# A second MoE layer's first tile: its tokens gathered from three of four batches, and the first half of its first product placed among the routing

## The chip, the cores and the metric

The kernel runs on one core of a Trainium2 chip. The metric is device time in microseconds (us), the median of several executions. The core has five instruction queues that matter here: PE (TensorE, matmuls and transposes), ACT (ScalarE), DVE (VectorE), POOL (GpSimd, which also issues the indirect gathers and scatters) and SP (SyncE, which issues all other transfers).

## The reference

Attention over four batches of 448 tokens (12 heads of 64, queries and keys normalised), then a dense two-layer MLP, called the first MoE here, then a routed MoE with eight experts:

```python
def _moe_ref(x, w_in, w_out):
    h = x @ w_in
    g = np.maximum(0.01 * h, h)
    return g @ w_out

def _moe2_ref(x, w_gate, w_output_gate, w1, w2):
    logits = x @ w_gate
    e_idx = np.argmax(logits, axis=1)
    probs = softmax(logits)
    gate_w = probs[np.arange(N), e_idx]
    eom = sigmoid(x @ w_output_gate)
    for e in range(E):
        mask = e_idx == e
        h = np.maximum(x[mask] @ w1[e], 0.0)
        out[mask] = gate_w[mask, None] * eom[mask, e, None] * (h @ w2[e])
    return out
```

There are 1792 tokens of width 768, and w1 and w2 are 768 x 1024 and 1024 x 768 for each expert.

## The kernel before, in words

Products in float32 are made from two halves: every operand is split into a rounded high part and the remainder, and three matmuls (high by high, remainder by high, high by remainder) replace one. A high part is a copy on ACT, a remainder (`lo_of`, line 63, whoever calls it) a subtraction on DVE.

**The first MoE's end.** Its last work is batch 3: the group "m2" of the last eighth of the hidden width, six units (one for each 128 columns of the result), each of six matmuls of 128x448 and one addition on DVE into `y` (line 727). In between lie the routing steps of batch 2, which `Route.steps` lists (`s2`): tables of token numbers (`tab`, line 885) and of gate weights (`stab`).

**Routing.** `Route` handles one batch. `logits` multiplies y by both gates; `read_logits` and `turn_logits` bring tokens onto partitions; `pick` takes the maximum and makes the one-hot (lines 807 to 815, DVE); `rank` counts with matmuls how many earlier tokens went to the same expert, over all batches so far (`cum`); `place` (843 to 849) splits that rank into a column, which is expert and chunk of 128, and a place within the chunk. `make` and `table` (876, 882) build a table with a row for each expert and chunk (112 rows = 8 experts x 14 chunks) and 128 places, as a matmul of two comparison matrices A and Bm. For the last batch (`late`) this is written out in the main function. `columns` transposes 128 columns of y and writes them to the DRAM tensor `x2d`, by SP (line 777).

Then the number of chunks of each expert (at least one) gives the order of the tile slots: `perm` (1159) picks from `tab` the rows that are alive, `idx` (1178) is the list of 128 token numbers for each slot, and `flags` (1189, 1190) say for each slot whether the expert changes and to which.

**The second layer.** `slot_tile(t)` handles 128 tokens: its tokens are gathered from x2d by POOL (`gather`, line 1171, three tiles ahead), transposed and split (`prep`, 1218), multiplied by w1 in two halves of 512 columns (`m1`, 1243, 18 matmuls each), passed through relu (1248), turned (`turn`, 1253) and multiplied by w2 in two halves of 384 columns (`m2`, 1259 to 1261, 24 matmuls each), scaled with the gate weights (`rsc`, 1312) and scattered to the output by POOL (1325). A slot with a new expert splits new weights (`wsplit`, 1211) and loads those of the next expert (968). The weights of the first expert are split by `high1` and `low1` (1104, 1109) around the routing; those of w2 at 1353 and 1361. Slot 0 also makes the gate weights of batch 3: `factors` (DVE, 1340 and 1341, after `weigh` and `weigh_more`, 855 to 865) and `weights_made` (PE, 1348).

**The order.** PE, ACT, DVE and POOL run their instructions in the order in which the function writes them (`manual_schedule`); only SP's order comes from a planner. Each waits where what it needs is not ready, and everything behind it on its queue waits too. Pools are stacked: a pool opened after another was closed takes over its room, and its first writer waits for the last users of what lay there. Slot 0's tokens are in x0, whose gather comes behind the indices and the whole of x2d:

```python
    pi = mm_small(tab, perm, P, NSLOT)
    idx = cst.tile([P, NSLOT], I32, name="idx")
    nc.vector.tensor_scalar(idx, pi, BIG, None, ALU.add)
    gather(0)
```

Of the kernel before, what the change touches and what calls it, by code (L numbers as in the profile page):

```python
# [20 lines left out]
def attention_moe_moe2(  # L21
# [33 lines left out]
    NSLOT = JMAX + NE - 1  # L55
    NSTAT = min(NSLOT, JMAX + NE // 2)
    K1 = D // P
# [74 lines left out]
    jexp = cst.tile([NE, 1], F32, name="jexp")  # L132

# [14 lines left out]
    sX, sR, sD = ExitStack(), ExitStack(), ExitStack()  # L148
    xT = []
    for i, st_ in enumerate((sX, sR)):  # L150
        px = st_.enter_context(tc.tile_pool(name=f"px{i}", bufs=1, side="right" if i else "left"))
        xT.append([px.tile([P, B // 2, NPAIR, S], F32R, name=f"xT{h}{i}") for h in "hl"])
# [591 lines left out]
    class Route:  # L744
# [5 lines left out]
        def bank(self, shape):  # L750
            return self.ps[0].tile(shape, F32, name="ch", bufs=self.ps[1])
# [9 lines left out]
        def columns(self, ds, own=None):  # L761
# [7 lines left out]
            for d, pt in zip(ds, pts):  # L769
# [7 lines left out]
                nc.sync.dma_start(rows, xn)  # L777

        def small(self, n, name):
            shape = [CP, NC, n] if n > 1 else [CP, NC]  # L780
            if self.kept and name in ("ids", "col", "pf", "d8", "z8", "z", "sm"):
                return cst.tile(shape, F32, name="k" + name)
# [124 lines left out]
    sA, sB, pA, pB, sG, sM, sW, sH = (ExitStack() for _ in range(8))  # L907
# [53 lines left out]
    pp = sY.enter_context(tc.tile_pool(name="pp", bufs=1, space=bass.MemoryType.PSUM, side="left"))  # L961
# [43 lines left out]
    nc.vector.tensor_scalar(place, iota[:CP], HALF, 1.0 / P, ALU.subtract, ALU.mult)  # L1005
    h4, h5, h6, h7 = (wts.half() for _ in range(4))
# [59 lines left out]
    one, two = Route(1, (pp, 1), rt), Route(2, (pp, 1), rt)  # L1066
# [24 lines left out]
    pc = pB.enter_context(tc.tile_pool(name="pc", bufs=2, space=bass.MemoryType.PSUM, side="right"))  # L1091
    late = Route(B - 1, (pc, 2), rt, kept=True)
    late.count()
    do(group("m2", NG - 1, B - 1), s2[5:11])
# [3 lines left out]
    w1h, w1l = [], []  # L1098
    wa = ctx.enter_context(tc.tile_pool(name="wa", bufs=1, side="left"))

    def high1(pool):
        c = len(w1h)
        w1h.append(pool.tile([P, F], F32R, name=f"w1h{c}"))
        nc.scalar.activation(w1h[c], r1[c // 2][:, c % 2], AF.Copy)  # L1104

    def low1(pool):
        c = len(w1l)
        w1l.append(pool.tile([P, F], F32R, name=f"w1l{c}"))
        lo_of(nc.vector, w1l[c], r1[c // 2][:, c % 2], w1h[c])

    for c in range(2):
        high1(wa)
    for d in range(KD):
        late.logits(d)
    for c in range(2):
        low1(wa)
    late.read_logits()
    late.columns((0,), own)
    late.turn_logits()
    late.columns((1, 2), own)  # L1120
    late.pick()
    for step in s2[11]:
        step()
    late.rank(last=True)
    late.columns((3, 4, 5), own)
# [276 lines left out]
```

## Time and profile before

| | us |
|---|---|
| median of three runs | 1156.8 |
| range of the three | 1155.01 to 1156.95 |
| the profiled execution | 1158.73 |
| its span in the trace | 1157.0 |
| PE busy in the span | 1113.9 (96%) |
| DVE busy | 780.4 (67%) |
| ACT busy | 497.7 (43%) |
| POOL busy | 388.8 (34%) |

The span runs from the first to the last instruction of the profiled execution; its own time is 1.73 us longer. Times of the trace count from the span's start. A view of the chain follows the work that ended last back to what released it; a timeline lists the instructions of an engine in order. In a timeline a line gives start, busy time, engine, line of the kernel, operation, result and operands, and their number; in brackets stands how long the engine was idle before, and whose work ended that. The granted clock is a share of 2.4 GHz.

### The profile page before, as it was taken

The page shows a single profiled execution, that of the slowest core. Times are in us where ns is not written, and L with a number is a line of the kernel's source. Part 1 is how long each engine was busy: PE and PEld are TensorE (multiplying, and loading weights), DVE is VectorE, ACT ScalarE, POOL GpSimd, SP SyncE. Part 2 cuts the span into 40 slices and gives each one's busy share as a digit, 9 for nine tenths or more (in the row PEclk, how much of TensorE's full clock was granted, in tenths as well). Part 3 has the DMA queues.
Part 4 walks back from the last instruction along what each step waited for, and adds up shares of the span by engine and source line. Part 5 has one row for each costly group of instructions (what it writes and reads, how often), then busy time and mean ns, then how long its engine had stood idle before and what let it go on. Part 6 is the DMA issues. An engine that isn't in the chain of part 4 may idle for free. (4 is left out here: it accounts for less than half of the span.)

```text
span 1157.0 us, 18278 instructions
## 1 busy us (share of the span) xinstructions
PE 1113.9 (96%) x6684; PEld 913.4 (79%) x6684; DVE 780.4 (67%) x1373; ACT 497.7 (43%) x791; POOL 388.8 (34%) x278
## 2 busy tenths in 40 slices
PE   6999999998999999999999999897799999999997
PEld 3555555554889999999999999796789989898996
DVE  7888878877787787778777776457561297116445
ACT  4666767665453222222222222225252287126444
POOL 3677787774233222222222322002121022102122
PEclk9999999999999999999999999999899999999999
DMA  5211221111222111121121210623752199105446
GB/s 145 81 55 51 73 67 54 25 39 50 56 82 69 55 56 55 55 54 56 46 63 42 57 54 28 238 70 79 293 196 93 34 331 372 52 23 192 173 164 240
DMA packets 68075, 116.21 MB, mean 100 GB/s; under 512 B 6780, under 2 KB 45948, under 8 KB 67968
## 3 DMA queue, kind: packets, MB, share of 16 engines
q1 hardware_dynamic: 64848, 103.87, 27.9%
q0 software_dynamic: 3120, 11.02, 2.7%
q8 instruction: 54, 0.88, 0.3%
q14 instruction: 53, 0.43, 0.1%
HBM read 106.61 MB, written 12.58 MB: 103 GB/s over the span
## 5 line engine op out<-in xcount | busy, mean ns | idle before, releaser
L657 POOL TENSOR_TENSOR raw<-raw,top 128x384 f32<-128x384 f32 x62 | 65.5, 1056 | 244.7 <-DVE raw L653 244.7
L693 PE MATMUL mo<-xTh,w0h 128*128 128x448 f32 x384 | 142.3, 371 | 0.8 <-DVE gl L63 0.8
L719 PE MATMUL mp<-gh,w1h 128*128 128x448 f32 x384 | 142.3, 370 | 0.0
L721 PE MATMUL mp<-gl,w1h 128*128 128x448 f32 x384 | 141.3, 368 | 0.0
L720 PE MATMUL mp<-gh,w1l 128*128 128x448 f32 x384 | 141.1, 367 | 0.0
L695 PE MATMUL mo<-xTh,w0l 128*128 128x448 f32 x384 | 141.0, 367 | 0.0
L694 PE MATMUL mo<-xTl,w0h 128*128 128x448 f32 x384 | 140.9, 367 | 0.0
L1325 POOL DMA_INDIRECT out_dram<-y,idx x18 | 36.2, 2008 | 270.4 <-DVEq L1320 155.2
L293 DVE TENSOR_REDUCE md<-tp 112x2 f32<-112x896 f32 x94 | 102.0, 1085 | 22.8 <-PE tp L291 22.5
L314 ACT ACTIVATE p<-sc 112x896 f32<-112x896 f32 x96 | 88.2, 918 | 59.6 <-PE sc L312 53.9
L727 DVE TENSOR_TENSOR y<-mp,y 128x448 f32<-128x448 f32 x168 | 101.4, 619 | 17.0 <-PE mp L721 16.8
L63 DVE TENSOR_TENSOR hL<-pt,hT 128x512 fp32r<-128x512 f32 x36 | 24.9, 692 | 117.4 <-ACTq L1279 60.6
L1259 PE MATMUL py<-w2h,hT 128*128 128x384 f32 x288 | 99.7, 346 | 0.0
L331 POOL TENSOR_TENSOR pr<-pr,p 112x896 f32<-112x896 f32 x43 | 91.4, 2126 | 17.2 <-ACT p L314 15.2
L1261 PE MATMUL py<-w2l,hT 128*128 128x384 f32 x288 | 96.6, 335 | 0.0
L1260 PE MATMUL py<-w2h,hL 128*128 128x384 f32 x288 | 96.5, 335 | 0.0
L702 ACT ACTIVATE g<-mo 128x448 f32<-128x448 f32 x64 | 34.9, 545 | 138.1 <-PE mo L695 138.1
L1243 PE MATMUL ph<-w1h,xgh 128*128 128x512 f32 x216 | 87.1, 408 | 0.0
L323 PE MATMUL av<-p,vv 112*64 112x448 f32 x384 | 86.3, 564 | 0.0
L1243 PE MATMUL ph<-w1l,xgh 128*128 128x512 f32 x216 | 84.8, 397 | 0.0
L1243 PE MATMUL ph<-w1h,xgl 128*128 128x512 f32 x216 | 84.6, 395 | 0.0
L693 PEld LDWEIGHTS mo<-xTh,w0h 128*128 128x128 f32 x384 | 72.1, 188 | 9.6 <-DVE gl L63 2.1
(235 smaller groups left out, 2421.8 us busy)
## 6 DMA issues: line engine op xcount, KB each, us to landing
r<-in_moe_w_dram SPq DMA_DIRECT2D x27, 1024.0 KB, 5.5
r<-in_moe_w_dram SPq DMA_DIRECT2D x36, 768.0 KB, 7.5
wd<-in_moe_w_in_dram SPq DMA_DIRECT2D x32, 384.0 KB, 3.2
wd<-in_moe_w_out_dram SPq DMA_DIRECT2D x32, 384.0 KB, 3.1
qk<-in_q_dram SPq DMA_DIRECT2D x24, 224.0 KB, 2.9
qk<-in_k_dram SPq DMA_DIRECT2D x24, 224.0 KB, 3.5
vv<-in_v_dram SPq DMA_DIRECT2D x24, 224.0 KB, 3.2
x2d<-xn SPq DMA_DIRECT2D x24, 224.0 KB, 3.1
```

The costliest lines, as they stand in the source:

```text
L293: nc.vector.tensor_reduce(st["md"][:, c, ::DH], sc[:CP, :, :S], AX.X, ALU.max)
L693: nc.tensor.matmul(ph, wh_[:, c], xh, start=(c == 0), stop=False)
L694: nc.tensor.matmul(ph, wh_[:, c], xl, start=False, stop=False)
L695: nc.tensor.matmul(ph, wl_[:, c], xh, start=False, stop=(c == KD - 1))
L719: nc.tensor.matmul(py, hi[:, sl], gh, start=(j == 0), stop=False)
L720: nc.tensor.matmul(py, lo[:, sl], gh, start=False, stop=False)
L721: nc.tensor.matmul(py, hi[:, sl], gl, start=False, stop=(j == GF - 1))
L727: nc.vector.tensor_tensor(y[b // 2][:, b % 2, d], py, y[b // 2][:, b % 2, d], ALU.add)
L1243: nc.tensor.matmul(ph[n], (xh, xl, xh)[k][:, c], (w1h, w1h, w1l)[k][c][:, s_], start=(c == 0 and k == 0), stop=(c == K1 - 1 and k == 2))
L1259: nc.tensor.matmul(py[n], hT[:, c], w2h[:, c, s_], start=(c == 0), stop=False)
L1260: nc.tensor.matmul(py[n], hL[:, c], w2h[:, c, s_], start=False, stop=False)
L1261: nc.tensor.matmul(py[n], hT[:, c], w2l[:, c, s_], start=False, stop=(c == K2 - 1))
```

## The change

- `first_tokens`: once batch 2 is in the table, row 0 of `tab` (the first 128 tokens of expert 0) is turned into indices by a matmul of one column, and POOL gathers these tokens into x0 from the first three batches of x2d. This lies between two halves of the third unit of the last product.
- `lacking`, `spare_slot`: if that row is not full, expert 0 gets one chunk more, and its later chunks move up by one slot; the number of possible slots goes from 21 to 22.
- The splits of the first expert's w1 (`high1`, `low1`) go partly into the last product and partly between the routing steps; they lie in the room of the first MoE's input (`held`), which is now kept, and in `wa`.
- x0's transposes and split (`prep0`) and the 18 matmuls of the first half of slot 0's first product (`m1_some`) go between the routing steps of batch 3; the columns of y are written to x2d one at a time there.
- All four Bm compares of batch 3 are made by DVE. The gate weights of batch 2 are no longer made in the last product: slot 0 makes those of batch 2 and slot 1 those of batch 3, both ahead of the second turn.
- w2's halves have a pool of their own (`ws`), six of its high parts are made before the relu; the loads of w2's last pair and of the second expert's w1 come behind the last write to x2d on SP.

The diff, cut to its core:

```diff
-    NSLOT = JMAX + NE - 1
+    NSLOT = JMAX + NE
     NSTAT = min(NSLOT, JMAX + NE // 2)
+    NB = (B - 1) * S
...
+    pq = ctx.enter_context(tc.tile_pool(name="pq", bufs=2, space=bass.MemoryType.PSUM, side="right"))
+    w1h, w1l, takes = [], [], [("mp", NU), ("ch", 1)]
+    rsc = cst.tile([P, NSLOT], F32, name="rsc")
...
+    held = [px.tile([P, 4 * F + D], F32R, name=f"h{h}", tag=f"xT{h}1") for h in "hl"]
+
+    def high1(room=None):
+        c = len(w1h)
+        w1h.append(room or held[0][:, c * F:(c + 1) * F])
+        nc.scalar.activation(w1h[c], r1[c // 2][:, c % 2], AF.Copy)
+
+    def low1(room=None):
+        c = len(w1l)
+        w1l.append(room or held[1][:, c * F:(c + 1) * F])
+        lo_of(nc.vector, w1l[c], r1[c // 2][:, c % 2], w1h[c])
+
+    xgh, xgl = ([t[:, 4 * F:].rearrange("p (c t) -> p c t", c=K1)] for t in held)
+    x0 = dec.tile([P, D], F32, name="x0", tag="wd", bufs=WD)
+    nc.gpsimd.memset(x0, 0.0)
+    late = Route(B - 1, bank, rt, kept=True)
+
+    def lacking():
+        nc.vector.tensor_reduce(few, tab[:1], AX.X, ALU.max)
+        nc.vector.tensor_scalar(few, few, -1.0, None, ALU.is_ge)
+        nc.vector.tensor_scalar(more[:1], few, float(P), HALF + P - 1, ALU.mult, ALU.add)
+
+    def first_tokens():
+        t = bank([P, S])
+        nc.tensor.matmul(t[:, 0:1], tab, ident[:NTAB, 0:1], start=True, stop=True)
+        nc.vector.tensor_scalar(idx0, t[:, 0:1], BIG, None, ALU.add)
+        nc.gpsimd.indirect_dma_start(
+            out=x0[:, :], out_offset=None, in_=x2d[:NB, :],
+            in_offset=bass.IndirectOffsetOnAxis(ap=idx0[:, 0:1].bitcast(U32), axis=0),
+            bounds_check=NB - 1, oob_is_err=False)
+
+    def spare_slot():
+        t = bank([P, S])
+        nc.tensor.matmul(t[:NTAB, 0:1], selr[:1], few, start=True, stop=True)
+        nc.vector.tensor_tensor(jrow, jrow, t[:NTAB, 0:1], ALU.add)
+
+    between = {2: [first_tokens]}
+    behind = {0: s2[5], 1: [*s2[6], s2[7][0], high1], 2: [lacking, high1], 3: [low1, high1],
+              4: [spare_slot, low1, high1]}
+    for unit in group("m2", NG - 1, B - 1):
+        (one_, two_), put = moe.second(*unit[1:])
+        one_()
+        for step in between.get(unit[2], ()):
+            step()
+        two_()
+        for step in behind.get(unit[2], ()):
+            step()
+        put()
...
+    h4, h5, l4, l5 = (wa.tile([P, F], F32R, name=f"w1{n}") for n in ("h4", "h5", "l4", "l5"))
+    high1(h4)
+    late.count()
     for d in range(KD):
         late.logits(d)
-    for c in range(2):
...
+    units = [(0, c) for c in range(K1)] + [(2, c) for c in range(4)] + [(1, c) for c in range(K1)] + [(2, 4), (2, 5)]
+
+    def m1_some(n):
+        for _ in range(n):
+            m10(*units.pop(0))
...
+    xlow = [prep0(0)]
+    late.columns((1,), own)
     late.pick()
-    for step in s2[11]:
-        step()
+    low1()
     late.rank(last=True)
-    late.columns((3, 4, 5), own)
+    high1(h5)
+    xlow.append(prep0(1))
     late.place(last=True)
-
...
+        nc.vector.tensor_scalar(Bm, place, late.pf[:, c:c + 1], None, ALU.is_equal)
...
+    late.spare(last=True)
+    for step in xlow:
+        step()
+    late.columns((4,), own)
+    m1_some(2)
...
-    gather(0)
...
+    m1_some(4)
+    low1(l4)
     pf_ = mm_small(ones_mat[:NE, :1], fl.rearrange("p a b -> p (a b)"), 1, 64)
-    late.spare(last=True)
-    flags = cst.tile([1, 64], I32, name="flags")
...
+    for t in (1, 2):
+        nc.gpsimd.memset(xg[t], 0.0)
+        gather(t)
+    nc.gpsimd.memset(xg[0], 0.0)
+    with tc.issue_after(late.sent.ins):
+        load2(0)[-1]()
+        for ld in load1(1):
+            ld()
+    for c in range(K2 // 2 + 2):
+        nc.scalar.activation(w2h[:, c], r2[c // 2][:, c % 2], AF.Copy)
+    m1_some(len(units))
+    nc.scalar.activation(hs[:, :F // 2], ph0, AF.Relu)
+    for c in range(K2 // 2):
+        lo_of(nc.vector, w2l[:, c], r2[c // 2][:, c % 2], w2h[:, c])
...
-            for c in range(K2 // 2, K2):
-                wsplit(r2, w2h, w2l, c)
-            for ld in load2(1):
-                ld()
-            for terms in ((0,), (1,), (2,)):
-                for c in range(K1):
-                    m1(0, c, terms)
...
-            factors()
+            for c in range(K2 // 2 + 2, K2):
+                nc.scalar.activation(w2h[:, c], r2[c // 2][:, c % 2], AF.Copy)
+            for c in range(K2 // 2, K2):
+                lo_of(nc.vector, w2l[:, c], r2[c // 2][:, c % 2], w2h[:, c])
+            for ld in load2(1):
+                ld()
+        if t < 2:
+            factors((two, late)[t])
         for c in range(2, K1):
             m1(1, c)
         relu(1)
         for c in range(4):
             m2(0, c)
+        if t < 2:
+            weights_made((two, late)[t])
         turn(1)
+        if t < 2:
+            pt = p2.tile([P, 3, P], F32, name="pt")[:, 0, :NSLOT]
+            nc.tensor.matmul(pt, stab, perm, start=True, stop=True)
+            nc.vector.tensor_copy(*((rsc[:, 1:], pt[:, 1:]) if t else (rsc[:, :1], pt[:, :1])))
         if nxt:
             with tc.If(chg == 1):
                 for c in range(3):
```

## Rows read from the trace of the kernel before

**Rows 1.** The page's part 1: busy us (share of the span) and instructions.

```profile
PE 1113.9 (96%) x6684; PEld 913.4 (79%) x6684; DVE 780.4 (67%) x1373; ACT 497.7 (43%) x791; POOL 388.8 (34%) x278
```

**Rows 2.** The chain in order of time, 802 to 893: start us, us, what.

```profile
802.98 3.45 DMA x2d<-xn
...
807.67 7.95 DMA x<-x2d,idx
...
817.27 6.63 PE ph L1243 x24
...
829.24 0.43 PE pt L1253 x4
...
831.76 0.89 PE pt L1348 x8
...
838.00 5.61 PE ph L1243 x24
...
892.93 5.61 PE ph L1243 x24
```

**Rows 3.** Timeline of PE, slot 0's transposes.

```profile
815.76 1.51 PE L1218 MATMUL pt<-ident,x 128*128 128x128 f32 x6 [9.56 <-DMA x<-x2d,idx]
```

**Rows 4.** Timeline of DVE, 789 to 829.

```profile
789.28 0.28 DVE L885 TENSOR_TENSOR tab<-ch,tab 112x128 f32<-112x128 f32 x1
...
795.71 2.36 DVE L63 TENSOR_TENSOR w1l<-r,w1h 128x1024 fp32r<-128x1024 f32 x2 [0.53 <-ACT w1h L1104]
...
797.99 0.18 DVE L807 TENSOR_REDUCE m<-lg 112x4 f32<-112x32 f32 x1
...
800.13 0.19 DVE L843 SCALAR_TENSOR_TENSOR t<-lg,oh 112x32 f32<-112x32 f32 x1 [0.86 <-PE lg L820]
...
801.84 1.34 DVE L876 TENSOR_SCALAR A<-iota,kcol,kids 112x112 f32<-112x112 f32 x1
...
804.26 0.29 DVE L885 TENSOR_TENSOR tab<-ch,tab 112x128 f32<-112x128 f32 x1
...
805.04 0.18 DVE L1178 TENSOR_SCALAR idx<-ch 128x21 int32<-128x21 f32 x1 [0.49 <-PE ch L1130]
...
806.74 4.64 DVE L63 TENSOR_TENSOR w1l<-r,w1h 128x1024 fp32r<-128x1024 f32 x4 [0.23 <-issue]
...
817.24 1.15 DVE L63 TENSOR_TENSOR xgl<-pt,xgh 128x384 fp32r<-128x384 f32 x2 [5.86 <-ACT xgh L1220]
...
818.31 7.03 DVE L63 TENSOR_TENSOR w2l<-r,w2h 128x768 fp32r<-128x768 f32 x8
...
825.86 0.18 DVE L855 TENSOR_REDUCE kz<-kz 112x4 f32<-112x32 f32 x1
...
828.30 0.34 DVE L1341 TENSOR_SCALAR y<-iota,kcol,kz 112x112 f32<-112x112 f32 x1
```

**Rows 5.** Timeline of ACT: w2's first splits, and the first switch of experts.

```profile
806.27 3.04 ACT L1353 ACTIVATE w2h<-r 128x768 fp32r<-128x768 f32 x4
...
849.90 2.94 ACT L1211 ACTIVATE w1h<-r 128x1024 fp32r<-128x1024 f32 x3
```

**Rows 6.** Timeline of POOL: the zeroing of x0 and of xg.

```profile
802.39 0.73 POOL L1166 MEMSET x<- 128x768 f32 x1
...
809.10 0.75 POOL L1355 MEMSET xg<- 128x768 f32 x1
```

**Rows 7.** Windows: us, PE, PEld, DVE, ACT, POOL busy, then granted PE clock, DMA.

```profile
743.00:746.97 3.97, 0.00 (x2) 0.00 (x1) 2.75 (x11) 1.46 (x4) 0.77 (x2) 1.00 0.46 116
...
746.97:750.40 3.43, 3.32 (x11) 2.84 (x12) 1.53 (x4) 0.66 (x2) 1.69 (x3) 0.55 0.00 0
...
805.30:819.30 14.00, 3.91 (x13) 2.90 (x14) 7.57 (x16) 6.44 (x10) 6.69 (x7) 0.51 0.75 282
```

**Rows 8.** The tile xg, 800 to 960: its gathers from issue to landing.

```profile
DMA to landing us min/median/max: 2.7/7.0/8.3
```

**Rows 9.** The tiles r, 800 to 840: loads of weights from issue to landing.

```profile
DMA to landing us min/median/max: 4.7/7.8/14.1
```

More of the change, by code (lines that the diff above doesn't have):

```diff
@@ L1113, in attention_moe_moe2, with prep0 @@
+    high1(h4)
+    late.count()
     for d in range(KD):
         late.logits(d)
-    for c in range(2):
-        low1(wa)
+    low1()
     late.read_logits()
+    def prep0(g):
+        pt = pp.tile([P, 3, P], F32, name="mt", tag="mp", bufs=NU)
+        for j in range(3):
+            nc.tensor.transpose(pt[:, j], x0[:, (3 * g + j) * P:(3 * g + j + 1) * P], ident)
+        hi, lo = xgh[0][:, 3 * g:3 * g + 3], xgl[0][:, 3 * g:3 * g + 3]
+        nc.scalar.activation(hi, pt, AF.Copy)
+        return lambda: lo_of(nc.vector, lo, pt, hi)
@@ L1118, in attention_moe_moe2, with m10 @@
+    ph0 = pq.tile([P, F // 2], F32, name="ph")
+    def m10(k, c):
+        nc.tensor.matmul(
+            ph0, (xgh, xgl, xgh)[k][0][:, c], (w1h, w1h, w1l)[k][c][:, :F // 2],
+            start=(k == 0 and c == 0), stop=(k == 2 and c == K1 - 1))
+    units = [(0, c) for c in range(K1)] + [(2, c) for c in range(4)] + [(1, c) for c in range(K1)] + [(2, 4), (2, 5)]
+    def m1_some(n):
+        for _ in range(n):
+            m10(*units.pop(0))
     late.columns((0,), own)
     late.turn_logits()
-    late.columns((1, 2), own)
+    xlow = [prep0(0)]
@@ L1121, in attention_moe_moe2 @@
+    late.columns((1,), own)
     late.pick()
-    for step in s2[11]:
-        step()
+    low1()
     late.rank(last=True)
-    late.columns((3, 4, 5), own)
+    high1(h5)
+    xlow.append(prep0(1))
     late.place(last=True)
-    def mm_small(lhsT, rhs, m, n):
-        t = pc.tile([P, S], F32, name="ch", bufs=2)
-        nc.tensor.matmul(t[:m, :n], lhsT, rhs, start=True, stop=True)
-        return t[:m, :n]
-    def places(c, engine):
+    m1_some(3)
+    late.columns((2,), own)
+    m1_some(3)
@@ L1141, in attention_moe_moe2 @@
     ni = cst.tile([NE, 1], I32, name="ni")
-    nc.vector.tensor_scalar(ni, late.cn, HALF + P - 1, None, ALU.add)
+    nc.vector.tensor_scalar(ni, late.cn, more, None, ALU.add)
     nc.vector.tensor_scalar(ni, ni, 7, None, ALU.arith_shift_right)
@@ L1145, in attention_moe_moe2 @@
     nc.vector.tensor_scalar(bn[:, 1:2], ni, jexp, 1.0, ALU.subtract, ALU.max)
-    for c in range(2, NC):
+    for c in hi:
         late.make(tab, late.ids, (c,), False)
-        places(c, nc.vector)
-    late.table(range(2))
-    br = pc.tile([P, S], F32, name="ch", bufs=2)
+        places(c)
+    late.table(lo)
+    late.columns((3,), own)
+    br = bank([P, S])
     nc.tensor.matmul(br[:NTAB, 0:1], after, bn[:, 1:2], start=True, stop=True)
     nc.tensor.matmul(br[:NTAB, 1:2], selr, bn[:, 1:2], start=True, stop=True)
-    late.table(range(2, NC))
+    late.table(hi)
     slot = cst.tile([NTAB, 1], F32, name="slot")
@@ L1297, in slot_tile @@
             m2(1, c)
-        if not t:
-            weights_made()
         if nxt:
@@ L1309, in slot_tile @@
             m2(0, c)
-        if not t:
-            pt = p2.tile([P, 3, P], F32, name="pt")[:, 0, :NSLOT]
-            nc.tensor.matmul(pt, stab, perm, start=True, stop=True)
-            nc.vector.tensor_copy(rsc, pt)
         for c in range(4, K2):
```

136 lines of the change are left out of this document (58 added, 78 removed).

## Prediction

> **What bounds it now.** I read the page first: of a span of 1157.0 us TensorE (PE) is busy 96% [rows 1]. An average that high hides the only place with slack, so the second view is the chain of work that ended last. From 838.00 on it is PE alone, one tile slot behind the other (first half product 24 matmuls in 5.61 us, 0.234 us each); ahead of that it leaves PE: the write of batch 3 to x2d (802.98 to 806.43), 1.24 us of queue work, the gather of the first 128 tokens (807.67 to 815.62), and only then PE again [rows 2]. The third view, PE in order of time, shows what that costs: PE sits idle 9.56 us until the gather lands and the transposes start at 815.76 [rows 3]. The fourth, VectorE (DVE) over the same stretch, shows what PE waited for before: each routing step waits for a DVE step [rows 4]. So the stretch from the first MoE's last product to the second slot (838.00) is bound by routing, write and gather, and not by PE. The slots behind it repeat every 18.31 us (838.00 to 892.93 are three [rows 2]) and the change leaves them as they are, but for slot 1.
>
> The sum is made against the profiled execution: 1158.73 us, which is its span of 1157.0 plus 1.73 around it, and 1.93 above the median of 1156.8. I work out by how much slot 1 starts earlier than 838.00, and what slot 1 then pays.
>
> **Removed: the gather's place on the chain.** Slot 0's tokens come out of batches 0 to 2 alone. Their table is added for batch 2 at 789.28 to 789.56 [rows 4]; the new one-column matmul and the index op follow at about 790. The last x2d write of batch 2 lands about then too. With the 1.24 us of queue work between a landed write and a gather's start [rows 2], the gather starts at 791.5. How long it takes is not shown for this spot: gathers landed between 2.7 and 8.3 us after their start [rows 8], the chain's own, beside weight loads, after 7.95 [rows 2]. No weight load is under way at 791, so I take the short end: landed at 794.2, at the long end 799.8. PE wants x0 at about 796.5, between turning the logits and the ranks. At the short end it costs nothing; at the long end 3.3 us, all of it on PE's queue in front of the rank matmuls. Its queue on POOL is empty: the two POOL compares are gone, and the zeroing of x0 is earlier.
>
> **Moved: the routing chain on DVE.** Before, two weight remainders (w1l, 2.36 us for two) ran until 798.07, and the maximum of the logits started at 797.99 behind them [rows 4]. After, the first two lie inside the last product, in the room of batch 2's weighting (some 3 us of small DVE ops and two table sums on PE, now moved to slot 0), and one of 1.18 us stays in front. With y's last addition done at 795.1 and the logits turned by 796.5, the maximum starts at 796.6: 1.4 us earlier. From there to the one-hot 1.1 us, as before: 797.7. Then the rank matmuls (1.06 us to the next DVE op before) run beside another remainder of 1.18 us: placing starts at 798.9, against 800.13.
>
> From placing to the finished table took 4.42 us (800.13 to 804.55). In it one comparison op, 0.3 us elsewhere, took 1.34 us, ending at 803.18; POOL's zeroing of x0 ended at 803.12 [rows 4, 6]. After, POOL computes nothing here, DVE does two more compares (estimated at 0.25 us each, since the factors' fourteen ops take 2.8): 0.75 + 8 x 0.25 + 0.5 + last table and addition 0.65 + 0.25 for waits = 4.15 at most, 3.9 without; I take 4.15 and the table is ready at 803.05. PE has columns and six of the first product's matmuls (1.4 us) to do meanwhile, in time it spent waiting. Next in the new order come the spare ops (0.2) and the two halves of xgl (1.15, as at 817.24) ahead of the indices: these end at 804.65 rather than 805.22. So most of what routing gains is spent on work that used to stand behind the gather.
>
> **Moved: what stands behind the indices.** DVE: offsets and flag rows 0.75, two remainders 2.36, flags 0.25 (808.0); four w2l at 0.88 (7.03 for eight) 3.5 (811.5); hL 0.7 (812.2); the other four w2l 3.5 (815.7); then the factors of batch 2, 2.8 us, as 825.86 to 828.64 before [rows 4]: 818.5. ACT: the last column copy (805.0), six w2h at 0.76 (3.04 for four) until 809.6, relu (estimated at 0.6), hT until 811.4, two w2h until 812.9 [rows 5]; it stays ahead of DVE. PE: of the 18 matmuls of the half product 12 lie among the routing; the last one waits for the second remainder at 807.7 and ends at 808.0. Then 18 of the other half (4.2), a turn 0.44 that waits for relu (810.3), half of the second product's half 2.1: PE is done at 815.65 and waits for the factors until 818.5. **DVE in its order is then what bounds slot 0**: a wait of 2.85 us replaces one of 9.56.
>
> From 818.5: weighting matmuls 0.89, turn 0.44, scale matmul 0.14 (an estimate from the 0.11 of a transpose), twelve matmuls 2.09 (829.67 to 831.76), transposes of slot 1's tokens 0.66 (four take 0.43), 24 matmuls 4.18 [rows 2]: 8.4, and slot 1 starts at 826.9 against 838.00: **11.1 us earlier**. The six transposes (1.51) and 24 matmuls that took 6.63 instead of 5.61 at the lower clock [rows 2, 3] are contained in that difference.
>
> **Added.** Slot 1 now has batch 3's factors and weighting: on PE 0.89 + 0.14 = 1.03 us on the path. The factors (2.8 us DVE) lie beside its matmuls, with some 3 us to spare; they also need slot 0's two y rooms empty, so its output written. If that cover is gone, they cost the time by which the write lands after about 836. The two one-column matmuls in the last product are 0.1 to 0.3; DVE has the 0.7 to hide them that the moved table sums leave. One slot more in the tail is a test that is not entered: nothing.
>
> **The held-back loads, and slot 1's gather.** Columns 3 to 5 are now written one by one, the last at 805.05; landed 3.45 later, 808.5, plus 1.24, a gather of 7.95 beside the loads [rows 2]: slot 1's tokens land at 817.7, or 818.1 with the longest landing. PE wants them at 822.1. The loads pass the read of the flags on SP's queue and start about 2.4 us earlier (from 808.0); were the write slowed by them, 4 us of room are there. Late next, after DVE, is this gather. The first of these loads, w2's last pair, feeds w2h's last two at 811.4. Issued at 805.6, with the shortest landing seen it is there at 810.3, with the middle one at 813.4 [rows 9], which costs DVE about 1; as first in its queue I take the short one.
>
> The sum: 11.1 - 1.03 = **10.1 us less**, 1158.73 to 1148.6; below the median as much: **1146.7 us**.
>
> **A rule weighed.** POOL's zeroing of xg and DVE's remainders fall together after 808. Before, four remainders took 4.64 us, 1.16 each, with a zeroing beside them at 809.10, no more than the 1.18 without one; the comparison op was held to the end of x0's zeroing [rows 4, 6]. The Trainium skill (SBUF — State Buffer, Who interferes with whom) says that VectorE in a two-port mode and GpSimd block each other for a whole instruction, that a VectorE op with two SBUF inputs is blocked only by a GpSimd op that reads SBUF. The trace agrees with both. By it an early zeroing of a gather room would hold a comparison once more: that is rival 3.
>
> **The rivals.**
> 1. PE's clock falls in the new wait. A wait of 3.97 us (743.00 to 746.97) was followed by 3.43 us at a granted 0.55, mostly the lower level of 1.2 GHz; 14 us about the 9.56 us wait stood at 0.51 [rows 7]. The new wait, 2.85 us, lies below both, with thinner waits ahead. The price by rows: 1.02 on 24 matmuls and 0.85 on transposes, 1.9 us: 1148.6. Chance 0.18.
> 2. A gather is late: x0 at its long end (3.3 us), or slot 1's beyond 822.1: up to 1150.0. For: 8.3 us has been seen [rows 8]. Against: x0 has no loads beside it. Chance 0.12.
> 3. A zeroing holds a comparison on the routing chain as at 802: 0.9 us, 1147.6. It is inside the forecast's own range. Chance 0.1.
> 4. DVE's order does not bind, because its small ops overlap more than I took: the 2.85 us go, 1143.9. Chance 0.08.
> 5. No gain: write, queue and gather of slot 1 stand in for those of slot 0, as if it landed after 832, when the 10 us are used up. It needs 14 us more than any row shows. Chance 0.03.
> 6. Slower: a nineteenth slot. If expert 0 had fewer than 128 tokens in batches 0 to 2, its first slot is not full and the change gives it a spare slot: 18.31 us, 1165.0. The point that decides is 128. For: expert 0 has just two slots (weights are switched at 849.90, in slot 1 [rows 5]), 129 to 256 tokens in four batches. Against: the reference's routing on its default inputs gives it 224, of these 164 in the first three batches, and the eight experts 2, 4, 1, 1, 5, 2, 2 and 1 slots, so that the first switch falls in slot 1, as in the trace. Chance 0.03.
>
> **How the numbers follow.** The forecast has what is left, 0.46: its time is 1146.7, its own range 1145.5 to 1148. For 8 in 10 I go from just below rival 4 (1143.5) to rivals 1 and 2 together (1146.7 + 1.9 + 3.3 = 1151.9). 0.2%, about what a measurement of this kernel tells from no change, is 2.3 us: faster by more than that holds in the forecast and rivals 1 to 4, 0.94, from which I take 0.04 for several of them at once with a wait on a reused room: 0.90. Within it 0.05, slower 0.05 (rival 6 and what rooms could add).
>
> **What would show it.** Right: PE's wait for x<-x2d,idx of 9.56 gone; half product matmuls between 799 and 808; indices near 804.7; a wait of 2 to 3 us in front of the weighting matmuls with DVE as releaser; slot 1 starting near 827; slot 1 some 1.0 longer than 18.31; 216 matmuls of the first product in all. Wrong: PE waiting for x0 ahead of the ranks (rival 2), slot 1's transposes waiting for a gather, a low clock at 818 (rival 1), w2h or hT waiting for a room, 228 matmuls (rival 6).

## The result, and the profile after

The changed kernel takes **1145.18 us** (median of 6 runs, 1143.65 to 1146.79), the kernel before in the same comparison 1157.3 (6 runs, 1155.01 to 1158.32): ratio 0.9901, interval [0.9889, 0.9912], 12.1 us less. The prediction was 10.1 less, to 1146.7, in a range from 1143.5 to 1151.9. Direction and size came out, and the sum behind them did not: it is short by 2.3 us in the part that the change rewrites, and some 4 us came from stretches whose instructions the change leaves alone.

The profiled execution of after took 1145.75 us, span 1143.8. The first MoE is called the first layer below. Cut at four marks that both traces have (the first matmul of the first layer's last group "m2", and the starts of slots 1, 2 and 17), the two spans differ like this:

| stretch, us | before | after | difference |
|---|---|---|---|
| start to the last group's first matmul | 784.72 | 780.62 | -4.10 |
| from there to slot 1 | 53.28 | 44.30 | -8.98 |
| slot 1 | 18.30 | 19.54 | +1.24 |
| slots 2 to 16 (15 slots) | 274.70 | 273.31 | -1.39 |
| slot 17 to the end | 26.00 | 26.03 | +0.03 |
| span | 1157.0 | 1143.8 | -13.2 |

The change itself is in rows two and three: 8.98 - 1.24 = 7.7 us. Since the two traces start 4.10 us apart, times around slot 0 are compared below as times after that first matmul, called the mark (784.72 before, 780.62 after).

The first part of the page of after, which answers to [rows 1]: PE's share of the span is up a point, its busy time 6 us down.

```profile
PE 1107.6 (97%) x6690; PEld 913.3 (80%) x6690; DVE 781.5 (68%) x1386; ACT 497.1 (43%) x791; POOL 389.6 (34%) x276
```

The chain in order of time, after (start us, us, what), which answers to [rows 2]. The write, the queue work and the gather are gone from it. What leads to slot 1 now is DVE, up to the factors, and then PE.

```profile
808.78 3.56 DVE w2l L64 x4
...
813.76 1.80 PE pt L1429 x8
815.56 0.44 PE pt L1337 x4
816.00 0.35 PE pt L1379 x2
816.36 0.50 PE py L1343
...
820.09 0.66 PE pt L1306 x6
...
824.92 5.57 PE ph L1327 x24
...
844.46 5.55 PE ph L1327 x24
...
862.69 5.57 PE ph L1327 x24
```

The timeline of PE, after [rows 3]: the transposes of x0 (L1168) wait for nothing, and the 9.56 us are gone. In their place stand three short waits, the longest 1.44 us in front of the weighting matmuls, with DVE as releaser. Slot 1's transposes (L1306) wait for nothing. The line below them is of PEld, the loading of weights into PE: the scale matmul's waits for DVE's addition to `stab`.

```profile
792.80 0.52 PE L1168 MATMUL mt<-ident,x 128*128 128x128 f32 x3
...
804.33 0.50 PE L1176 MATMUL ph<-w1l,hh 128*128 128x512 f32 x1 [0.30 <-DVE w1l L64]
...
806.80 0.66 PE L1337 MATMUL pt<-ident,hs 128*128 128x128 f32 x4 [0.62 <-ACT hs L1293]
...
813.76 1.80 PE L1429 MATMUL pt<-y,y 112*112 112x128 f32 x8 [1.44 <-DVE y L1421]
...
819.93 0.82 PE L1306 MATMUL pt<-ident,xg 128*128 128x128 f32 x6
```

```profile
815.95 0.30 PEld L1379 LDWEIGHTS pt<-perm,stab 112*128 112x128 f32 x2 [0.18 <-DVE stab L1430]
```

The timeline of DVE, after [rows 4]: one comparison took 0.96 us where the next one takes 0.32, and from the remainders of w2 on DVE hardly pauses until the last factor.

```profile
793.00 0.19 DVE L811 TENSOR_REDUCE m<-lg 112x4 f32<-112x32 f32 x1
...
795.88 0.96 DVE L880 TENSOR_SCALAR A<-iota,k3col,k3ids 112x112 f32<-112x112 f32 x1
...
796.83 0.32 DVE L880 TENSOR_SCALAR A<-iota,k3col,k3ids 112x112 f32<-112x112 f32 x1
...
799.76 0.29 DVE L889 TENSOR_TENSOR tab<-cb,tab 112x128 f32<-112x128 f32 x1
...
804.40 3.54 DVE L64 TENSOR_TENSOR w2l<-r,w2h 128x768 fp32r<-128x768 f32 x4
808.17 0.69 DVE L64 TENSOR_TENSOR hL<-pt,hT 128x512 fp32r<-128x512 f32 x1 [0.23 <-ACT hT L1338]
808.78 3.56 DVE L64 TENSOR_TENSOR w2l<-r,w2h 128x768 fp32r<-128x768 f32 x4
...
814.71 0.33 DVE L1422 TENSOR_SCALAR y<-iota,k2col,k2z 112x112 f32<-112x112 f32 x1
```

The timeline of POOL, after [rows 6]: the gather of x0, the zeroing that runs beside that comparison, and slot 1's gather.

```profile
788.08 1.41 POOL L1131 DMA_INDIRECT x<-x2d,mrow  x1 [6.13 <-DVE y L729]
796.04 0.73 POOL L1283 MEMSET xg<- 128x768 f32 x1 [6.56 <-PE mt L1168]
805.91 2.92 POOL L1238 DMA_INDIRECT xg<-x2d,idx  x1 [9.14 <-DVE w2l L64]
```

Windows of after around the weighting (us, then PE, PEld, DVE, ACT, POOL busy, granted PE clock, DMA), which answer to [rows 7]: from 816 to 820 PE was busy throughout at a granted 0.57, mostly the lower level of 1.2 GHz.

```profile
816.00:820.00 4.00, 4.00 (x16) 3.96 (x16) 0.76 (x2) 0.60 (x1) 0.00 (x0) 0.57 1.01 395
820.00:825.00 5.00, 5.00 (x33) 4.96 (x32) 1.07 (x3) 1.45 (x3) 0.00 (x0) 1.00 1.01 392
```

### The profile page after: what moved, and what is told of

Same layout as the page of the kernel before. It is cut to its first block, busy times and chain, and to the rows that moved or that the text cites. A ratio compares the mean times of both kernels' runs of the same rounds, so it can differ in the third digit from the quotient of the medians.

```text
span 1143.8 us, 18349 instructions
## 1 busy us (share of the span) xinstructions
PE 1107.6 (97%) x6690; PEld 913.3 (80%) x6690; DVE 781.5 (68%) x1386; ACT 497.1 (43%) x791; POOL 389.6 (34%) x276
## 5 line engine op out<-in xcount | busy, mean ns | idle before, releaser
L723 PEld LDWEIGHTS mp<-gl,w1h 128*128 128x128 f32 x384 | 72.7, 189 | 6.1 <-DVE gl L64 0.4
L721 PEld LDWEIGHTS mp<-gh,w1h 128*128 128x128 f32 x384 | 72.7, 189 | 6.0 <-ACT gh L706 0.4
L697 PEld LDWEIGHTS mo<-xTh,w0l 128*128 128x128 f32 x384 | 72.1, 188 | 6.5 <-DVE w0l L64 0.5
```

The lines of the kernel that those rows point to most:

```text
L697: nc.tensor.matmul(ph, wl_[:, c], xh, start=False, stop=(c == KD - 1))
L721: nc.tensor.matmul(py, hi[:, sl], gh, start=(j == 0), stop=False)
L723: nc.tensor.matmul(py, hi[:, sl], gl, start=False, stop=(j == GF - 1))
```

## The experiments

Each was compared with the kernel before on the same chip. Three questions stood open: is the early gather what carries the gain; what did the wait for the factors cost, and can it be had back; and where do 4 us in untouched code come from.

**Both kernels once more.** No edit.

> The kernel before once more, unchanged, for its trace. In the two traces so far the last group of the first MoE's products starts at 784.72 (before) and at 780.62 (after), 4.1 us apart, although the code ahead of it is the same in both. If that is a difference of two executions, it starts here within 1 us of the repeated kernel after. If it belongs to the kernels (where their tiles lie), it starts near 784.7 again, about 4 us behind the repeated kernel after. From there to the second tile slot 53.3 us.

> The changed kernel once more, unchanged. From the start of the last group to the second slot 44.3 us, slot 1 19.5 us, in either case. If the 4.1 us ahead of the last group belong to the kernel, the group starts near 780.6; if to the execution, within 1 us of the repeated kernel before, and the ratio comes nearer to 1 - 7.8/1157 = 0.993.

Before: 1156.22 us, 53.06 us from the mark to slot 1, a slot 18.31. After: 1143.5 (1141.25 to 1145.4), ratio 0.9887 [0.9865, 0.9909], 44.02 us, slot 1 19.54, later slots 18.22. So these lengths repeat to some 0.3 us, and the 7.7 us of the changed part are 53.06 - 44.02 - 1.23 = 7.8 here. What varies from execution to execution lies in two places. One is the attention: its last exponential ends at 291.26 us before and 289.06 after, and at 289.01 and 287.22 in the repetitions. The other is what follows PE's wait of some 4 us between 738 and 747, which every trace has: in the 6 us behind it the granted clock was 0.50 after, but 0.72 before and in the repetition of after, and the stretch is about 1 us longer for it. The 4.10 us of the table's first row are thus 2.2 of the attention, 2.9 of the first layer (see the address runs), and 1.0 the other way.

**The early gather undone.** The first 128 tokens are gathered behind the final indices again, their transposes and the half product behind that; the rest is the changed kernel.

```
-    between = {2: [first_tokens]}
+    between = {}
...
+    nc.gpsimd.indirect_dma_start(out=x0[:, :], in_=x2d[:, :], ... ap=idx[:, 0:1] ...)
...
-    m1_some(len(units))
+    for g in range(2):
+        prep0(g)()
+    m1_some(len(units))
```

> Kernel after with one part undone: slot 0's tokens are gathered behind the final indices and the whole of x2d, as before the change, and its transposes, split and the first half of its first product stand behind that gather; all else (weights' splits, held-back loads, factors) is as in the kernel after. Theory (the early gather carries the gain): the gather starts 25.3 us after the start of the last group, lands 7 to 8 us later, and PE waits some 8 us for it; slot 1 starts 52 to 55 us after the start of the last group instead of 44.2, 1152 to 1155. Rival (the new order of splits and loads carries it, the gather was hidden anyway): 44 to 47 us, 1144 to 1147.

1160.25 us (1159.51 to 1162.91), ratio 1.0039 [1.0024, 1.0053]: slower than the kernel before. The chain in order of time has the gather and the transposes of x0 back:

```profile
806.97 7.12 DMA x<-x2d,idx
814.22 1.51 PE pt L1157 x6
...
839.56 5.57 PE ph L1316 x24
```

PE waited 10.7 us for x0, and slot 1 began 59.17 us after the mark (780.39) instead of 44.30, some 4 us beyond what was expected. A granted 0.50 from 805 to 818 and a wait of 1.5 us for the factors are among it; it was not taken apart further. The early gather, with the transposes and the half product that it lets go ahead, carries the gain, and more than all of it: with the rest of the change alone the kernel is 3 us slower than before.

This run also shows a wait as long as the 1.44 us of the changed kernel with no lower clock behind it. PE waits 1.47 us for the factors, in front of the same matmuls, and the clock stays at 1.00:

```profile
830.02 1.71 PE L1418 MATMUL pt<-y,y 112*112 112x128 f32 x8 [1.47 <-DVE y L1411]
```

```profile
831.70:835.70 4.00, 4.00 (x28) 3.79 (x27) 1.13 (x4) 1.21 (x3) 0.00 (x0) 1.00 0.26 104
```

**The factors left out.** Batch 2's factors and weighting are left out of slot 0, to see what they cost in all.

```
-        if t < 2:
-            factors((two, late)[t])
+        if t == 1:
+            factors(late)
...
-        if t < 2:
-            weights_made((two, late)[t])
+        if t == 1:
+            weights_made(late)
```

> Kernel after without batch 2's gate weights: slot 0 leaves out their factors (DVE, ACT) and their weighting matmuls, the rest is as in the kernel after; the weights of batch 2 are missing in the output. Theory: all that this step costs on the path goes, wait 1.44, weighting 1.8 and half clock 1.6, with the relu that stood behind its exponentials some 0.5 more: slot 1 starts 5.0 to 5.5 us earlier, 39 us after the start of the last group, 1139.9 us. Rival (only its PE work is on the path): 0.9 to 1.8 us, 1143.5 to 1144.3.

1141.09 us (1140.62 to 1142.2), ratio 0.9863 [0.9846, 0.9879]; 39.28 us from the mark to slot 1, 5.0 less than the changed kernel. The median fell by less, since the first layer of this build stands at the slow pace that the address runs below are about (445.0 us). The clock stayed at 1.00 from 812 to 820. So factors, weighting and the slow matmuls behind them are worth 5 us of path, of which 0.9 is the weighting itself. The scale matmul, at its place behind the turn but with no weighting ahead, takes 0.14 us of the chain here and not 0.35.

**The weighting put later.** Its matmuls behind the first twelve of the second product's other half, the scales before the last twelve; the factors stay where they are.

```
-        if t < 2:
-            weights_made((two, late)[t])
...
         for c in range(4):
             m2(1, c)
+        if not t:
+            weights_made(two)
...
         for c in range(4, K2):
             m2(0, c)
+        if not t:
+            scales()
```

> Kernel after, but in slot 0 the weighting matmuls of batch 2 stand behind the first twelve matmuls of the second half product, and the scale matmul ahead of the last twelve, as they stood before the change. Theory (DVE's factors are what PE waits for in slot 0, and the lower clock behind that wait costs again): the 1.44 us wait, some 0.9 us of stretched weighting matmuls and 1.6 us of half clock go, slot 1 starts 3.5 us earlier (40.8 us after the start of the last group), about 1141.7 us. Rival (the gather of slot 1 bounds slot 0): its transposes then wait for the gather, no gain, 1145. Rival (the clock falls anyway, for the work ahead of the wait): 1.5 to 2 us gained, 1143.4.

1142.91 us (1142.56 to 1143.93), ratio 0.9879 [0.9862, 0.9895]; 41.58 us. The longest wait left is the turn's, and it is shorter than in the changed kernel and no lower clock follows it (timeline of PE, and a window):

```profile
814.30 0.66 PE L1337 MATMUL pt<-ident,hs 128*128 128x128 f32 x4 [0.89 <-ACT hs L1332]
```

```profile
814.30:817.00 2.70, 2.69 (x18) 2.70 (x19) 2.43 (x10) 0.60 (x1) 0.30 (x1) 1.00 1.02 406
```

That 0.89 comes of an order on ACT: the second relu stood behind the factors' exponential, which waits for DVE. Hence 41.58 and not the 40.8 expected.

**The factors later too.** They are issued behind the second turn, the weighting behind the third quarter of the second product, the scale last.

```
-        if t < 2:
-            factors((two, late)[t])
+        if t == 1:
+            factors(late)
...
         turn(1)
+        if not t:
+            factors(two)
...
         for c in range(4, K2):
             m2(0, c)
+        if not t:
+            weights_made(two)
```

> As the earlier run with the late weighting, but slot 0's factors of batch 2 come behind the second turn on DVE and ACT, the weighting matmuls behind the third quarter of the second product, and the scale matmul last. Theory: nothing on PE waits for the factors any more; relu no longer stands behind their exponential: slot 1 starts 0.6 to 1.2 us earlier than in that run (41.58 us after the start of the last group), at 40.4 to 41.0. Rival (PE then waits for DVE's remainder of the second turn or the factors all the same): 41.6 or more.

**1140.55 us** (1139.67 to 1140.86), ratio 0.986 [0.9843, 0.9876]: faster than both kernels, its interval below the one of the changed kernel's result ([0.9889, 0.9912]; that of the repetition, [0.9865, 0.9909], begins inside it). Slot 1 starts 40.37 us after the mark (779.13), and takes 0.11 us more. The weighting waits for nothing and takes 0.94 us in the chain, and PE is busy in the whole window ahead of it, at the full clock:

```profile
816.32 0.94 PE pt L1439 x8
...
819.50 5.67 PE ph L1327 x24
...
839.15 5.55 PE ph L1327 x24
```

```profile
812.00:816.30 4.30, 4.30 (x28) 3.92 (x27) 4.05 (x17) 1.14 (x4) 0.04 (x1) 1.00 1.03 406
```

So 44.30 - 40.37 = 3.9 us of the changed kernel's path (3.7 against its repetition) were a wait, and the slower work behind it, that another order avoids.

**The held-back loads let go.** The order that issues them after the last x2d write is taken out.

```
-    with tc.issue_after(late.sent.ins):
+    if True:
```

> The changed kernel without the order that holds expert 0's last second-layer load and the next expert's first loads back until the last x2d write of batch 3 has been sent; nothing else differs. Theory: the order is not needed for the time. In the changed kernel slot 1's gather lands at 812.7 and its transposes want it at 819.9, 7 us of room, and the x2d writes land in 2.8 to 3.1 us. Even if the writes now stood behind eight weight loads (0.4 us or so each on SP's queue), the gather would still be there in time: 44.3 us from the last group of first-layer products to slot 1 as in the changed kernel (44.0 to 44.3 in two runs), 1144 to 1146 us. A gain would show as an earlier w2 load and a shorter wait in front of the weighting matmuls, 1 us at most. Rival: the loads take the DMA engines from the x2d writes and from the gather, the gather lands after 820 and PE waits for it in front of slot 1's transposes: 1147 or more, with 46 us or more in the trace.

1147.69 us (1146.22 to 1149.09), ratio 0.9933 [0.9917, 0.995]; 46.74 us from the mark (778.83). Slower by 2.4 us in the trace. The rival had the time and its first half, the loads slow the x2d writes, but not the place: slot 1's transposes waited for nothing. SP's queue, and ACT and PE behind it:

```profile
788.87 0.37 SPq L972 DMA_DIRECT2D r<-in_moe_w_dram  x1
791.60 1.61 SPq L781 DMA_DIRECT2D x2d<-xn  x2
793.49 0.45 SPq L972 DMA_DIRECT2D r<-in_moe_w_dram  x1
795.95 3.67 SPq L781 DMA_DIRECT2D x2d<-xn  x3
799.71 0.59 SPq L972 DMA_DIRECT2D r<-in_moe_w_dram  x1
800.39 0.56 SPq L781 DMA_DIRECT2D x2d<-xn  x1
```

```profile
807.75 0.60 ACT L1338 ACTIVATE hT<-pt 128x512 fp32r<-128x512 f32 x1 [2.76 <-DMA r<-in_moe_w_dram]
```

```profile
813.96 2.10 PE L1429 MATMUL pt<-y,y 112*112 112x128 f32 x8 [2.65 <-DVE y L1422]
```

The next expert's first loads now go ahead of w2's last pair, which is third (799.71), and of the writes; x2d's writes land 5.3 us after their issue instead of 2.9 (medians). The last write, issued at 800.39, lands 7.2 us later, at 807.6; in the changed kernel the last one takes 3.1 and lands at 804.95. ACT's hT waits for all of batch 3's writes before it writes its room, and here it stands until the last of them has landed: it starts at 807.75, 28.9 us after the mark instead of 26.9, and with it DVE and the weighting. The line above puts this wait down to a load, but w2's last pair had landed at 806.9, and the next load lands at 810.1; the last of hT's semaphores to be set is that of the write. PE's wait grows from 1.44 to 2.65. The held-back loads are thus a part of the gain: the order spares the writes to x2d, and what waits for these is not the gather but hT's room.

**Where untouched code got faster.** The changed kernel has 96 bytes less of constants at the bottom of the state buffer, so that the turned tokens of batches 0 and 1 lie at byte 23328 and not 23424 of a partition. The first run gives the kernel before those 96 bytes less (256 out, 160 in), the second gives the changed kernel 96 bytes more.

```
+    cst.tile([P, 40], F32, name="pad")
...
-    fl = cst.tile([NE, 2, 32], F32, name="fl")
+    fl = selr[:, :64].rearrange("p (a b) -> p a b", a=2)
```

> Kernel before with one thing moved: the pool of constants is 96 bytes smaller, so that the first MoE's input xT of batches 0 and 1, and all that lies above it on that side of SBUF, lies 96 bytes lower, just where the kernel after has it. Theory (the pace of the first MoE's matmuls follows where their operand lies): its stage, from the first to the last copy of a hidden block, takes 442.7 us as in the kernel after instead of 445.6, the rest as before: 2.9 us less, 1153.2. Rival (the 2.9 us come from another thing that the change moved, the order of SP for one): 445.6, no change, 1156.1.

```
+    cst.tile([P, 24], F32, name="pad")
```

> Kernel after with 96 bytes added to the constants, so that xT of batches 0 and 1 lies where the kernel before has it. Theory: the first MoE's stage takes 445.6 us instead of 442.7; from the last group to the second slot 44.2 us as before; 2.9 us more, 1147.0. Rival: 442.7 and 1144.1.

The kernel before with less: 1152.03 us (1150.2 to 1154.6), ratio 0.9958 [0.9945, 0.997], and the first layer, from the first to the 61st of its 64 hidden copies (the expectations call that one the last), 442.75 us instead of 445.54. The changed kernel with more: 1146.73 (1145.77 to 1149.23), ratio 0.9912 [0.9895, 0.9928], and 445.41 instead of 442.61. The stage moved as expected in both; behind the 61st copy comes PE's wait of 4 us. The time of the first run fell by more than the 2.9 us expected, by 5.1 from 1157.17: its later slots are shorter too, by 2.3 us from slot 1 to slot 17. So moved rooms alone, with no other edit, are worth 5 us in the kernel before. ACT's copies show it unit by unit; between the two lines of a pair lie 18 matmuls of 448 columns. Kernel before, batches 2 and 3 (3.70 us apart), then 0 and 1 (3.65 here, 3.72 in other groups):

```profile
513.18 0.55 ACT L702 ACTIVATE g<-mo 128x448 f32<-128x448 f32 x1 [7.68 <-PE mo L695]
...
516.88 0.55 ACT L702 ACTIVATE g<-mo 128x448 f32<-128x448 f32 x1 [0.73 <-PE mo L695]
...
527.83 0.55 ACT L702 ACTIVATE g<-mo 128x448 f32<-128x448 f32 x1 [2.04 <-PE mo L695]
...
531.48 0.55 ACT L702 ACTIVATE g<-mo 128x448 f32<-128x448 f32 x1 [1.42 <-PE mo L695]
```

Changed kernel, the same: 3.70, and 3.60.

```profile
509.81 0.54 ACT L704 ACTIVATE g<-mo 128x448 f32<-128x448 f32 x1 [7.76 <-PE mo L697]
...
513.51 0.55 ACT L704 ACTIVATE g<-mo 128x448 f32<-128x448 f32 x1 [0.73 <-PE mo L697]
...
524.45 0.55 ACT L704 ACTIVATE g<-mo 128x448 f32<-128x448 f32 x1 [2.04 <-PE mo L697]
...
528.05 0.55 ACT L704 ACTIVATE g<-mo 128x448 f32<-128x448 f32 x1 [1.37 <-PE mo L697]
```

The later slots are another matter: 18.22 us with the 96 bytes and without, against 18.31 before, and 18.17 in the kernel before with less. Addresses alone can shorten them, as the last shows; which of the moved rooms did it in the changed kernel was not tried.

**What it is about the address.** Three more builds, from the version of 1140.55 us, move the tokens of batches 2 and 3 (at 96 bytes past a multiple of 128; those of batches 0 and 1 at 32; the weights that lie on the right-hand side at 0). First 64 bytes under the tokens, which move the weights too:

```
+    ctx.enter_context(tc.tile_pool(name="pad", bufs=1, side="right")).tile([P, 16], F32, name="pad")
     xT = []
```

> The version with the late weighting (1140.55 us), with 64 unused bytes added at the bottom of the right-hand side of the state buffer, so that the turned tokens of batches 2 and 3 lie 64 bytes lower (186272 instead of 186336; 32 bytes past a multiple of 128, as those of batches 0 and 1 do); the weights on that side move by 64 too. Theory, that a matmul's pace hangs on the byte address of its operand: the 18 matmuls of a first product of batches 2 and 3 fall from 3.70 to 3.60 us, as those of batches 0 and 1 did when the 96 bytes went; 32 such units, about 2.9 us less, 1137.7 us, and the stage of the first layer from its first to its last hidden copy shrinks from 442.7 to about 439.8. Rival: the 3.60 belongs to the distance between operands or to one place only; units of batches 2 and 3 stay at 3.70 and the time at 1140 to 1141, or the moved weights cost elsewhere and it is longer.

1146.22 us (1145.2 to 1146.84), ratio 0.9914 [0.9897, 0.993]: the theory falls. Batches 2 and 3 stay at 3.70 us, batches 0 and 1, whose tokens did not move, go from 3.60 to 3.68, and the stage takes 446.05. It is not the tokens' address alone. (All spans of the stage run to the 61st copy.) The next pair of runs: pads under and over the tokens, so that only they move against 128 (room for it by letting small constants share a tile), and a pad over them alone.

```
+    ctx.enter_context(tc.tile_pool(name="pad", bufs=1, side="right")).tile([P, 16], F32, name="pad")
     xT = []
...
+    ctx.enter_context(tc.tile_pool(name="pad2", bufs=1, side="right")).tile([P, 16], F32, name="pad2")
     dec = sD.enter_context(tc.tile_pool(name="dec", bufs=1, side="right"))
```

> The version with the late weighting (1140.55 us) with three small constants sharing rooms of others, so that everything lies 128 bytes lower, and with 64 of those bytes put below and 64 above the turned tokens of batches 2 and 3: these alone move against a multiple of 128, from 96 to 32 bytes past it, as batches 0 and 1 lie; all weights stay at their place against 128. The run with one pad has shown that 32 bytes alone are not enough: with the weights moved by 64 too, the first products of all batches stood at 3.68 to 3.70 us. Theory: the fast pace is a matter of the pair, operand and weights, of which 32 and 0 bytes past a multiple of 128 is a fast one; all 18-matmul units of first products stand at 3.60 us, half of them 0.1 us less than before, 2.9 us in all: 1137.7 us, and 439.8 from the first to the last hidden copy. Rival: the pace hangs on something else that went with the moves (the place of a whole pool, the rooms of other engines' operands); the units of batches 2 and 3 stay at 3.70, time 1140 to 1142, or it is longer.

> The version with the late weighting with one pad of 64 bytes above the turned tokens of batches 2 and 3: tokens of batches 0 and 1 stay at 32 and those of 2 and 3 at 96 bytes past a multiple of 128, the weights go from 0 to 64. Theory, distance: what counts is the distance between tokens and weights; batches 0 and 1 go from 32 to 96 and so from 3.60 to 3.70 us, batches 2 and 3 from 96 to 32 and so from 3.70 to 3.60: the stage of the first products stays at about 442.7 and the time at 1140 to 1141. Rival, the pair itself: 32 and 0 is fast, no other; all units at 3.68 to 3.70, the stage at 446 and the time at 1144.

With both pads the units of batches 2 and 3 go to 3.60 us as well (ACT's copies, that version):

```profile
507.21 0.55 ACT L706 ACTIVATE g<-mo 128x448 f32<-128x448 f32 x1 [7.59 <-PE mo L699]
...
510.81 0.55 ACT L706 ACTIVATE g<-mo 128x448 f32<-128x448 f32 x1 [0.63 <-PE mo L699]
```

and the stage takes 440.43 us, 2.3 less than 442.73, where 2.9 was expected. The time is 1139.53 (1137.38 to 1148.49), ratio 0.9878 [0.9835, 0.992]: the profiled execution is the one of 1137.38, one of the four took 1148.49 and left no trace, and by its runs this version can't be told from the one of 1140.55. With the upper pad alone, 1146.35 us in a single run, the stage 447.3, batches 0 and 1 at 3.68 and 2 and 3 at 3.72 but for the first units. So the distance falls too. Of the pairs of tokens and right-hand weights that were run, 32 with 0 gave 3.60; 0 with 0, 96 with 0, 32 with 64 and 96 with 64 gave 3.64 to 3.72. The run without factors agrees: its tokens of batches 0 and 1 lie at byte 23264, at 96 as well, and their units take 3.70. Why is not shown, nor what the weights on the other side do to it.

## Why the prediction was right, and where its sum was not

Point by point, times after the mark.

**The bound and the wait that goes**: right. PE's 9.56 us [rows 3] are gone, and undoing that one part gives more than the whole gain back.

**x0's gather**: right that nothing waits, though by 0.3 us and with luck: it took 4.4 us and not 2.7. It was there 11.9 us after the mark, and PE came to its transposes at 12.2, where 11.8 had been predicted.

**The routing chain**: the maximum was predicted at 11.9 and came at 12.4; the table at 18.3, and it was finished at 19.4. Of these 1.1 us about 0.5 are **rival 3**: the comparison at 795.88 ended at 796.84, the zeroing beside it at 796.77, and the next comparison of its kind, which takes 0.32, started 0.95 us after it, where the last two start 0.44 apart. The rest is the later maximum. That it was the zeroing is read from the two ends; no run moves it. The Trainium skill (SBUF — State Buffer, Who interferes with whom) has VectorE in a two-port mode and GpSimd block each other for a whole instruction; the 0.96 beside the zeroing agrees, as the 1.34 of before did [rows 4].

**DVE's order then bounds slot 0**: right, and its terms held. From the table to the last factor 15.45 us were predicted (18.33 to 33.78) and 15.0 measured (19.43 to 34.42). PE waited 1.44 us and not 2.85, because it came 0.8 later itself and because the weighting's first matmuls did not wait for the last factor; that changes nothing, as the end of the weighting, predicted at 34.67, came at 34.94.

**From the weighting to slot 1**: this is the step that failed. Its terms were turn 0.44, scale matmul 0.14, twelve matmuls 2.09, transposes 0.66 and 24 matmuls 4.18, together 7.51 us; the trace took 9.36. The twelve matmuls took 3.73 (816.36 to 820.09), 1.64 more, at a granted 0.57: **rival 1** came about, at 1.64 where its price was 1.9. It had 0.18, because the wait was to be shorter than the 3.97 us of [rows 7]. That row shows a wait that was enough, not one that was needed. In the runs, waits of 1.44 (after, its repetition and the one with 96 bytes more) and 2.65 us were followed by a granted 0.57 to 0.71 in a stretch of 4 us behind the weighting, the 0.89 of the late weighting by 1.00, and so was the 1.47 of the run with the early gather undone. So a wait of 1.4 us was enough in three traces and not in a fourth, and what made the difference is not shown. In the repetition the low clock begins earlier, and the twelve matmuls take 2.85.

The other 0.21 is the scale matmul, 0.35 and not 0.14. The estimate was right for the matmul: before, it took 0.14 in the chain.

```profile
835.66 0.14 PE pt L1312 x2
```

What the prediction left out is that it now stands 0.44 us behind the weighting, whose sums DVE must first add to `stab` (815.60 to 815.89); the load of `stab` into PE waits 0.18 us for that. Without the weighting, at the same place, it takes 0.14 again. The same 0.21 makes slot 1 longer by 1.24 instead of 1.03 (0.88 + 0.35).

**The held-back loads and slot 1's gather**: right on the loads' first, which came 5.6 us after its issue at 802.73 and cost ACT 0.18; taking the order away costs 2.4. Slot 1's gather was issued at 805.91; the trace has 15 of its 16 ends, the last at 814.3, and it was wanted at 819.9: the room was some 5.6 us, not 4. (The 6.8 us that give the 812.7 in the expectations belong to a later gather.)

**No nineteenth slot**: right. Rivals 2, 4 and 5 did not come about.

**The sum**: of the 10.1 us, 7.7 came from the changed part. The 2.3 that lack are the clock (1.64), the scale matmuls (0.4), and what is left of the routing's delay at the end of the weighting (0.27). Against that stand 2.9 us in the first layer, of which the prediction said nothing, and 1.4 in the later slots, of which it had said that "the change leaves them as they are". It read the diff as instructions; it is also a list of rooms, and a few small tiles less moved everything above them on that side. The first layer's part is shown by the 96 bytes, in both directions; what shortened the later slots is not. By medians 7.8 + 2.9 + 1.4 = 12.1. The forecast fell into its range because the two misses have opposite signs.

## What to carry to other kernels

When a long wait goes, look for the short one that takes its place, and move what it waits for behind matmuls that don't need it: here a wait of 1.44 us, with the slow matmuls behind it, was worth 3.9 us, and the version that gave PE other work there beats both kernels. Compare the addresses of two builds before a difference in untouched code is put down to chance or to the change, and ask of a matmul-bound stage whether its pace per unit is the same for all rooms. And give the low clock a real chance behind a wait on PE that is shorter than those already seen to be followed by it, for a row that shows a longer wait says nothing of a shorter one: here waits of 1.4 us were followed by it in three traces and not in a fourth. Where a wait is put down to a transfer, compare when that transfer landed: in the run with the loads let go it was another.

## What the hardware showed that was not expected

- The same 18 matmuls take 3.60 or 3.64 to 3.72 us by the byte address of tokens and weights against 128. A shift of 96 bytes was worth 2.8 us of 445.5 (first to 61st copy) in two kernels, in both directions.
- PE's granted clock stood at 0.57 from 816 to 820, behind a wait of 1.44 us and a weighting that stretched over 1.80 us because it followed DVE's ops one by one. A wait of 1.47 us in another run was followed by 1.00.
- POOL's gather instruction for slot 1 took 2.92 us where those behind it take 1.62 and 1.00; it started while DVE worked on w2l. In the run with the loads let go it started beside hL and took 1.00. But the one of 1.62 started beside w2l too, and in the kernel before one that started beside w1l (810.12) took 1.01, so the cause is open. Nothing waited for it, and it was not tried further.
